# The first group's w_in, fetched and rounded among the first four pieces, with its products from the fourth piece on

## The chip, the cores and the metric

The kernel runs on one core of one Trainium2 chip. The metric is the device time of one execution in microseconds. The kernel before took 1035.81 us, the median of three runs (1035.71 to 1037.92). The profiled execution took 1034.46 us, and its span from the first to the last instruction was 1032.7 us.

## The reference

Two blocks follow each other. The first is a retention layer (attention with a decaying causal mask instead of a softmax), the second a feed-forward layer with the activation h * erf(softplus(h)).

```python
# q, k, v: (8 batches, 8 heads, 576 tokens, 64)
scores = (1 / sqrt(64)) * q @ k.T
Dmat   = where(i >= j, gamma[head] ** (i - j), 0)
x      = (scores * Dmat) @ v                 # -> (4608 tokens, 512)
# w_in: (512, 2048), w_out: (2048, 512)
h   = x @ w_in
sp  = maximum(h, 0) + log1p(exp(-abs(h)))
out = (h * erf(sp)) @ w_out
```

All inputs are random, in float32. The two weights reach the kernel as float64, seen as pairs of 32-bit words, and the kernel rounds them to float32 itself.

## The kernel before

**Attention by pieces.** The 4608 tokens are cut into 36 pieces of 128. A piece goes through three stages: `transposes` (called T below), `scores` (S) and `outputs` (O). Four pieces make a chunk of 512 tokens, which is an input x of the feed-forward layer. There are nine chunks. Pieces 0 to 7 are transposed on TensorE; from piece 8 on VectorE does it (`SQUARES = 8`).

```python
def transposes(i):                       # T(i)
    ...
    for name in "qk":
        pt = ps_at.tile(...)
        for p in range(NP):
            nc.tensor.transpose(pt[:, p, :], ..., ident)
        nc.scalar.copy(out=tT..., in_=pt...)      # qT, kT
    load(i + 2, "q")

def scores(i):                           # S(i)
    ...  # 8 matmuls kT x qT into two PSUM tiles
    for e in range(2):
        tt(sT[:, e], ps[e], mask..., ALU.mult)    # VectorE, "sT"

def outputs(i):                          # O(i)
    ...  # sT x v, and qT x state where a state exists, and k x v for the next state
    scaled(1)                            # VectorE: x <- o
    ...                                  # VectorE: sums; GpSimd: state
    scaled(0)                            # VectorE: x <- o
    load(i + 3, "kv")

stages = [(transposes, 0), (scores, 0)]
for i in range(len(pieces)):
    stages += [(transposes, i + 1), (outputs, i), (scores, i + 1)]
    if i in (PC + 1, 2 * PC - 1):
        stages[-3:-1] = stages[-2], stages[-3]
```

**Weights by parts.** The hidden dimension is cut into four groups. A group has four parts of w_in (tile `wa`) and four of w_out (`wb`), 512 KB each. `load_weights()` asks for the next part; `round_weights(n)` emits the next n steps of the rounding. One part is five steps; after the last part of a tile four more form sums in place.

```python
def load_weights():
    part = next(coming, None)
    if part is not None:
        t = wraw.tile([P, 2 * WP], UINT32, tag="wraw", name="wraw")     # 4 buffers
        for rows, src in part[0]:
            nc.sync.dma_start(out=t[rows]..., in_=src)
        words.append((t, *part[1:]))

def rounding():
        ...
        nc.scalar.activation(a_f, high_f, AF.Abs)                    # step 1, ScalarE
        nc.scalar.mul(out=r_f, in_=low, mul=2.0**-52)
        yield
        nc.vector.tensor_scalar(...)                                 # step 2
        yield
        nc.vector.tensor_scalar(...)                                 # step 3
        yield
        nc.vector.scalar_tensor_tensor(...)                          # step 4
        yield
        nc.vector.tensor_scalar(out=high, ...)                       # step 5
        engine = nc.vector if (name, g) == ("wa", 0) else nc.gpsimd
        engine.tensor_tensor(out=r_f, in0=high_f, in1=r_f, op=ALU.mult)
        engine.tensor_tensor(out=a_f, in0=a_f, in1=r_f, op=ALU.add)
        ...
        yield
        # after a tile's last part: four tt(...) that form the sums
```

So a part of the first group's w_in is two operations on ScalarE and six on VectorE; a part of w_out is two on ScalarE, four on VectorE and two on GpSimd.

**The first chunk's products.** `First.plain()` multiplies the first chunk with the first group's w_in in eight products of four matmuls (128x256 each). The first four need only w_in's first two parts, the last four the other two.

```python
for half, slots in enumerate(((A11, S3), (A12, A22))):
    for n in range(4):
        tok, f = n // 2, n % 2
        ...  # 4 matmuls into acc[n], from wa[slots[f]] and half the chunk's tokens
        if half == 1:
            nc.scalar.copy(out=(self.t2 if tok else self.t1)[:, f], in_=acc[n])
        yield
```

**The opening.** The order of everything up to the end of piece 7's scores is one string: `a` is the next attention stage, `p` one of the eight products (P below), `w` asks for a weight part, a digit is that many steps of rounding, `k` is two matmuls that only keep TensorE busy, `l` loads piece 2's k and v, `c` loads the second half of the constants, `s` stores chunk 0.

```python
load(0)
cst = ...;  nc.sync.dma_start(out=cst[:, :CONST_FIRST], ...)
...
load(1)
...
keep_busy(9)
weigh_values(0)
products = firsts[0].plain()
for what in "alkakakawkakakawaa3awwa2aaa5aawwa5pap5ppwwca4pa5pa5paa5ps1":
    if what == "a":
        attend(done[0] + 1)
    elif what == "p":
        next(products)
    ...
```

**The steady part.** Afterwards first and second products of successive chunks alternate, with attention stages between them as long as there are any. `operands_x` forms the operands of a chunk by four VectorE operations on 128x512.

```python
elif n + 2 < n_s:
    f = firsts[n + 1]
    for step, _ in enumerate(b.middle()):
        attend(min(done[0] + 1, most[0]))
        if step == 0:
            f.erf()
        elif step == 1 and n + 2 >= n_ch:
            operands_x(*order[n + 2])
        ...
    if n + 2 < n_ch:
        attend(after_chunk(n + 2))
        operands_x(*order[n + 2])
```

Of the kernel before, what the change touches and what calls it, by code (L numbers as in the profile page):

```python
# [54 lines left out]
def kernel(  # L55
# [15 lines left out]
    n_ch = n_tok // TCH  # L71
# [26 lines left out]
    def tt(out, in0, in1, op):  # L98
        nc.vector.tensor_tensor(out=out, in0=in0, in1=in1, op=op)  # L99
# [22 lines left out]
    def load_squares(i, name, src):  # L122
        t = raw.tile([P, NP, P * D // SQ], FP32, tag=name + "s", name=f"raw_{name}s", bufs=2)
        for b, s0, n, r0 in pieces[i]:
            m = n // SQ * D
            for part in range(P // SQ):
                e, d0 = part // 2, part % 2 * SQ
                tokens = src[b, e * NP : (e + 1) * NP, s0 : s0 + n, :].rearrange("p (r a) d -> r p (a d)", r=SQ)
                at = r0 // SQ * D
                nc.sync.dma_start(  # L130
                    out=t[part * SQ : (part + 1) * SQ, :, at : at + m - SQ], in_=tokens[:, :, d0 : d0 + m - SQ]
                )
        return t

    def load_rows(i, name, src, bufs):
        if name == "q":
            t = raw.tile([P, NP, P * D // SQ], FP32, tag="qs", name="raw_q", bufs=bufs)
            t = t.rearrange("p a x -> p (a x)")[:, : H * D].rearrange("p (h d) -> p h d", h=H)
        else:
            t = raw.tile([P, H, D], FP32, tag=name, name=f"raw_{name}", bufs=bufs)  # L140
        for b, s0, n, r0 in pieces[i]:
            for e in range(2):
                heads = src[b, e * NP : (e + 1) * NP, s0 : s0 + n, :]
                nc.sync.dma_start(out=t[r0 : r0 + n, e::2, :], in_=heads.rearrange("h p d -> p h d"))  # L144
        return t

    def load(i, names="qkv"):
        if i < len(pieces):
            t = loaded.setdefault(i, {})
            for name in names:  # L150
                src = {"q": q, "k": k, "v": v}[name]
                if name == "q" and i < SQUARES:
                    t["q"] = load_rows(i, "q", q, 2)
                elif name == "q":
                    t["qs"] = load_squares(i, "q", q)
                    t["ks"] = load_squares(i, "k", k)
                elif name == "v" or len(pieces[i]) == 1:
                    t[name] = load_rows(i, name, src, 4)
# [7 lines left out]
    gk, gq, gp, tri, gk2, gq2, tri2 = (cst[:, a:b] for a, b in zip(ends, ends[1:]))  # L166
    gq, gq2 = (g.rearrange("p (a i) -> p a i", a=NP) for g in (gq, gq2))
    gp = gp.unsqueeze(2).to_broadcast([P, NP, D])
    load(1)

# [52 lines left out]
# [3 lines that stand above are left out]
            t = wraw.tile([P, 2 * WP], UINT32, tag="wraw", name="wraw")  # L228
            for rows, src in part[0]:
                nc.sync.dma_start(out=t[rows].rearrange("p (h f) -> p h f", h=2), in_=src)  # L230
            words.append((t, *part[1:]))
# [48 lines left out]
    def round_weights(n=1):  # L280
        for _ in range(n):
            next(round_step, None)

    ident = cpool.tile([P, P], FP32, name="ident")
    make_identity(nc, ident)
    assert S % P == D and 2 * D == P and n_tok == len(pieces) * P and len(pieces) % PC == 0
# [139 lines left out]
    stages = [(transposes, 0), (scores, 0)]  # L426
# [4 lines left out]
    stages = [(of, i) for of, i in stages if i < len(pieces)]  # L431
    done = [0]

    def before_chunk(c):

        return stages.index((outputs, c * PC)) if c < n_ch else len(stages)

    def after_chunk(c):

        return stages.index((outputs, (c + 1) * PC - 1)) + 1  # L440

    def attend(upto):
        while done[0] < min(upto, len(stages)):
            of, i = stages[done[0]]
            of(i)
            done[0] += 1
# [3 lines left out]
    def load_x(g, c):  # L450
        x[g, c] = x_tile()
        nc.sync.dma_start(out=x[g, c][:, :n_dc], in_=xd[c])

    def store_x(c):
        nc.sync.dma_start(out=xd[c], in_=x[0, c][:, :n_dc])

    def operands_x(g, c):
        t = x[g, c]
        b11, b12, b21, b22 = (t[:, 2 * d : 2 * d + 2, h * TH : (h + 1) * TH] for d in range(2) for h in range(2))
        t1, t2, t4 = (t[:, n_dc + j, :].rearrange("p (d i) -> p d i", d=2) for j in range(3))  # L460
        if g == 0 or c == 0:
            tt(t1, b12, b11, ALU.subtract)
            tt(t2, b22, t1, ALU.subtract)
            tt(b12, b22, b12, ALU.subtract)
        else:
            tt(t2, b12, b11, ALU.add)
            tt(t1, b22, t2, ALU.subtract)
        if g == 0:
            store_x(c)
        tt(t4, b21, t2, ALU.subtract)  # L470
        x[g, c] = {A11: b11, A12: b21, S4: b22, A22: t4, S1: t1, S2: t2, S3: b12}
# [211 lines left out]
    order = [(g, c) for g in range(n_g) for c in range(n_ch)]  # L683
# [11 lines left out]
    def keep_busy(n):  # L695
        for _ in range(n):
            nc.tensor.matmul(idle[:, :P], lhsT=ident, rhs=ident, start=True, stop=True)
# [4 lines left out]
    def run(steps, rounds=(), stages=1):  # L702

        for step, _ in enumerate(steps):
            attend(min(done[0] + stages, most[0]))
            round_weights(rounds[step] if step < len(rounds) else 0)
# [4 lines left out]

    for what in "alkakakawkakakawaa3awwa2aaa5aawwa5pap5ppwwca4pa5pa5paa5ps1":
        if what == "a":
            attend(done[0] + 1)
        elif what == "p":
            next(products)
        elif what == "s":
            store_x(0)  # L720
        elif what == "l":
            load(2, "kv")
        elif what == "c":
            nc.sync.dma_start(out=cst[:, CONST_FIRST:], in_=consts[:, CONST_FIRST:])
        elif what == "w":
            load_weights()
        elif what == "k":
            keep_busy(2)
        else:
            round_weights(int(what))  # L730
    firsts[0].softplus()
    most[0] = before_chunk(3)
    attend(after_chunk(1) + 1)
    operands_x(0, 1)
    for step, _ in enumerate(firsts[1].first()):
        attend(done[0] + 1)
# [4 lines left out]
    for b, nxt in zip(blocks[1:], blocks[2:] + [None]):  # L741
        n = order.index((b.g, b.c))
        if isinstance(b, First):
            most_g[0] = order[n - 1][0] + 1
            run(b.middle(), (1, 1) if n != 2 else ())
            firsts[n - 1].sums()
            run(seconds[n - 1].first(), (1, 1) if n > 2 else ())
            run(b.last(), (1,) if 2 < n < n_ch else ())
            if n in (2, 3):
                load_weights()  # L750
            most[0] = before_chunk(n + 3)
# [3 lines that stand above are left out]
                attend(min(done[0] + 1, most[0]))  # L755
                if step == 0:
                    f.erf()
                elif step == 1 and n + 2 >= n_ch:
                    operands_x(*order[n + 2])
                elif step == 2 and n_ch - 4 < n < n_ch:  # L760
                    round_weights()
            if n + 2 < n_ch:
                attend(after_chunk(n + 2))
                operands_x(*order[n + 2])
            run(nxt.first(), (1,) if n > 1 else ())
            f.multiply()
            seconds[n + 1].begin()
            if n_ch <= n + 3 < n_s:
                load_x(*order[n + 3])
            run(b.last(), (0, 1) if n > 1 else ())  # L770
        elif n + 1 < n_s:
            firsts[n + 1].erf()
            seconds[n + 1].begin()
            rest = b.rest()
            for _ in range(3):
                next(rest)
            firsts[n + 1].multiply()
            run(rest)
            firsts[n + 1].sums((0,))
            first = nxt.first()  # L780
            next(first)
            firsts[n + 1].sums((1,))
            run(first)
        else:
            run(b.rest())
# [30 lines left out]
```

## Time and profile before

| What | Value |
|---|---|
| Time, median of three | 1035.81 us |
| Span of the profiled execution | 1032.7 us |
| TensorE busy | 1015.1 us (98%) |
| VectorE busy | 679.1 us (66%) |
| ScalarE busy | 387.8 us (38%) |
| GpSimd busy | 125.4 us (12%) |
| HBM read, written | 119.02 MB, 47.19 MB |

The shares are averages over the whole span. The opening is the first 70 us of it, and there the engines stand otherwise than later, so it has to be read by itself: the span in 40 slices, then the instructions of each engine in order of time. In those lists a row gives start, duration, engine, line, operation and tiles, and in brackets how long the engine was idle before it and what released it. Line 99 is the helper `tt`, so its groups are told apart by their tiles. TensorE is PE, VectorE DVE, ScalarE ACT, GpSimd POOL; SPq is the queue that issues the transfers.

### The profile page before, as it was taken

The numbers are of one execution on the slowest core, as the hardware profiler recorded it, in microseconds if no ns is written. First come the engines' busy times: TensorE is split into PE (matmuls) and PEld (weight loads), VectorE is DVE, ScalarE is ACT, GpSimd is POOL, SyncE is SP. The second block draws the span as 40 slices with busy tenths as digits, with TensorE's granted clock in tenths as the row PEclk, the third lists the DMA queues.
The fourth block names the chain that finished last, engine by engine and source line by source line (L and its number), as shares of the span: only waits on it lengthen the run. The fifth ranks groups of instructions, "written<-read, shape, count | busy, mean of one in ns | idle before, by whom it ended". The sixth has DMA issues, their size and how long they took to land.

```text
span 1032.7 us, 15920 instructions
## 1 busy us (share of the span) xinstructions
PE 1015.1 (98%) x6322; PEld 872.7 (85%) x6322; DVE 679.1 (66%) x1063; ACT 387.8 (38%) x477; POOL 125.4 (12%) x122
## 2 busy tenths in 40 slices
PE   8899999999999999999999999999999999999998
PEld 7777888887888788888888888888888888888887
DVE  3998877877875755666666656666657655555555
ACT  2353134232244444333443344444443333333332
POOL 2161121222211210000001001100100000000000
PEclk9999999999999999999999999999999999999999
DMA  8989979979983544444445344444333334444433
GB/s 192 213 212 228 244 159 241 230 173 247 216 195 131 184 143 143 142 143 165 163 155 169 145 143 143 151 166 153 143 122 122 123 124 131 132 130 133 126 89 116
DMA packets 148778, 167.27 MB, mean 162 GB/s; under 512 B 97632, under 2 KB 123360, under 8 KB 140640
## 3 DMA queue, kind: packets, MB, share of 16 engines
q1 hardware_dynamic: 147696, 165.47, 57.2%
q8 instruction: 50, 0.82, 0.4%
q10 hardware_dynamic: 1008, 0.79, 0.3%
q14 instruction: 24, 0.20, 0.1%
HBM read 119.02 MB, written 47.19 MB: 161 GB/s over the span
## 4 chain that ended last, share of the span: by engine, by line
PE 87%; DVE 4%; SPq 3%; DMA 3%; issue 1%; ACT 1%; POOL 0%; DVEq 0%; ACTq 0%
PE a L591 23%; PE a L483 22%; PE g L483 12%; PE g L591 11%; PE e L591 6%; PE e L483 5%; PE s L339 3%; PE o L357 2%; SPq L144 2%; PE o L380 1%; DMA wraw<-in_moe_w_in_dram 1%; PE o L368 1%; SPq L130 1%; DVE t L99 1%; DMA cst<-in_decays_dram 1%
## 5 line engine op out<-in xcount | busy, mean ns | idle before, releaser
L483 PE MATMUL a<-x,wa 128*128 128x256 f32 x1120 | 266.1, 380 | 0.0
L483 PEld LDWEIGHTS a<-x,wa 128*128 128x128 f32 x1120 | 211.6, 190 | 29.5
L591 PE MATMUL a<-wb,s 128*128 128x256 f32 x864 | 205.7, 381 | 0.0
L591 PEld LDWEIGHTS a<-wb,s 128*128 128x128 f32 x864 | 162.9, 190 | 23.6 <-ACT o L605 0.7
L99 DVE TENSOR_TENSOR t<-g,t 128x512 f32<-128x512 f32 x70 | 48.3, 690 | 150.6 <-ACT t L513 112.9
L483 PE MATMUL g<-x,wa 128*128 128x256 f32 x560 | 133.2, 381 | 2.0 <-DVE o L99 2.0
L483 PEld LDWEIGHTS g<-x,wa 128*128 128x128 f32 x560 | 105.7, 190 | 17.3 <-DVE o L99 2.4
L99 DVE TENSOR_TENSOR o<-a,o 128x512 f32<-128x512 f32 x108 | 74.3, 688 | 50.4 <-PE a L591 50.4
L508 ACT COPY t<-a 128x512 f32<-128x512 f32 x35 | 20.5, 586 | 189.8 <-PE a L483 189.8
L99 DVE TENSOR_TENSOR t<-t,s 128x1024 f32<-128x1024 f32 x72 | 87.8, 1260 | 0.0
L552 ACT ACTIVATE s<-t 128x1024 f32<-128x1024 f32 x72 | 72.1, 1049 | 32.3 <-DVE t L99 32.3
L267 POOL TENSOR_TENSOR wraw<-wraw 128x512 f32<-128x512 f32 x28 | 29.7, 1062 | 434.8 <-DVE wraw L265 182.5
L99 DVE TENSOR_TENSOR x<-x 128x512 f32<-128x512 f32 x116 | 79.7, 720 | 1.2
L519 ACT COPY t<-a 128x512 f32<-128x512 f32 x35 | 20.5, 586 | 151.9 <-PE a L483 151.9
L556 ACT ACTIVATE s<-s 128x1024 f32<-128x1024 f32 x72 | 72.1, 1048 | 0.4
L591 PE MATMUL a<-wb,t 128*128 128x256 f32 x288 | 68.6, 381 | 1.1 <-DVE t L99 1.1
L591 PE MATMUL e<-wb,t 128*128 128x256 f32 x288 | 68.6, 381 | 0.0
L591 PE MATMUL g<-wb,s 128*128 128x256 f32 x288 | 68.6, 381 | 0.0
L591 PE MATMUL g<-wb,t 128*128 128x256 f32 x288 | 68.2, 380 | 0.0
L99 DVE TENSOR_TENSOR o<-g,o 128x512 f32<-128x512 f32 x72 | 49.3, 685 | 28.1 <-ACT o L605 23.3
L483 PE MATMUL e<-x,wa 128*128 128x256 f32 x280 | 66.8, 381 | 0.0
L99 DVE TENSOR_TENSOR sT<-s,cst 128x512 f32<-128x512 f32 x72 | 46.1, 682 | 27.4 <-PE s L339 18.8
(75 smaller groups left out, 1199.9 us busy)
## 6 DMA issues: line engine op xcount, KB each, us to landing
od<-o SPq DMA_DIRECT2D x54, 512.0 KB, 3.6
x<-xd SPq DMA_DIRECT2D x27, 1024.0 KB, 4.8
o<-od SPq DMA_DIRECT2D x27, 1024.0 KB, 5.0
raw_qs<-in_q_dram SPq DMA_DIRECT2D x96, 112.0 KB, 4.7
raw_ks<-in_k_dram SPq DMA_DIRECT2D x96, 112.0 KB, 4.2
xd<-x SPq DMA_DIRECT2D x9, 1024.0 KB, 5.4
raw_k<-in_k_dram SPq DMA_DIRECT2D x64, 128.0 KB, 4.6
raw_v<-in_v_dram SPq DMA_DIRECT2D x64, 128.0 KB, 4.6
```

The lines of the kernel that those rows point to most:

```text
L99: nc.vector.tensor_tensor(out=out, in0=in0, in1=in1, op=op)
L130: nc.sync.dma_start(out=t[part * SQ : (part + 1) * SQ, :, at : at + m - SQ], in_=tokens[:, :, d0 : d0 + m - SQ])
L144: nc.sync.dma_start(out=t[r0 : r0 + n, e::2, :], in_=heads.rearrange("h p d -> p h d"))
L267: engine.tensor_tensor(out=r_f, in0=high_f, in1=r_f, op=ALU.mult)
L339: nc.tensor.matmul(ps[e][:, p, :], lhsT=t["kT"][heads[e], p, :], rhs=t["qT"][heads[e], p, :], start=True, stop=True)
L357: nc.tensor.matmul(o[p % 2][heads[(e + p) % 2], p // 2, :], lhsT=t["v"][:, 2 * p + e, :], rhs=t["sT"][:, e, p, :], start=(p < 2), stop=(no ...
L483: nc.tensor.matmul(acc[:, j * TH : (j + 1) * TH], lhsT=weights["wa", self.g][:, a, d, j * P : (j + 1) * P], rhs=x[self.g, self.c][a][:, d, :],
L508: nc.scalar.copy(out=self.t1[:, 1], in_=self.a)
L519: nc.scalar.copy(out=self.t2[:, 0], in_=self.a)
L552: nc.scalar.activation(self.s[:, j], t, AF.Softplus)
L556: nc.scalar.activation(self.s[:, j], self.s[:, j], AF.Erf)
L591: nc.tensor.matmul(acc[:, tp, :], lhsT=left[:, j * TH + tp * P : j * TH + (tp + 1) * P], rhs=weights["wb", self.g][:, b, j, :], start=(sta ...
```

## The change

The first two parts of w_in are asked for right after the constants, one ahead of piece 1 and one behind it; the other two follow after the first and second outputs. The rounding is spread among the first four pieces. The first chunk's products begin right after the fourth piece's outputs, and then alternate with the stages of pieces 4 to 7, where before they began after the fifth piece's scores and stood partly in a row. The rounding of w_out that stood behind piece 7's scores comes ahead of piece 6's outputs. The aim is to use VectorE while the first pieces are still arriving, and to give TensorE products to do between the stages of attention.

A second edit concerns the steady part: once no stage of attention is left, `operands_x` comes one step earlier, ahead of an addition of the second products. A set records which chunks have been done.

```diff
-    load(1)
 ...
+    load_weights()
+    load(1)
+    load_weights()
     ident = cpool.tile([P, P], FP32, name="ident")
 ...
+    summed = set()
+
     def operands_x(g, c):
+        summed.add((g, c))
 ...
-    for what in "alkakakawkakakawaa3awwa2aaa5aawwa5pap5ppwwca4pa5pa5paa5ps1":
+    for what in "alka1kak4awka1kak4awaa1a4aa1a4pawpawpap4awpa5wpapa5cpa5aa1s":
 ...
-                elif step == 1 and n + 2 >= n_ch:
+                elif step == 1 and (n + 2 >= n_ch or done[0] == len(stages)):
                     operands_x(*order[n + 2])
 ...
-            if n + 2 < n_ch:
+            if order[n + 2] not in summed:
                 attend(after_chunk(n + 2))
                 operands_x(*order[n + 2])
```

Written out with T, S, O and P, r for rounding steps and W for a part asked for, the two strings are:

```
before T0 S0 T1 O0 W S1 T2 O1 W S2 T3 r3 O2 W W S3 r2 T4 O3 S4 r5 T5 O4 W W S5 r5 P O5 P r5 P P
       W W T6 r4 P S6 r5 P T7 r5 P O6 S7 r5 P r1
after  T0 S0 r1 T1 r4 O0 W S1 r1 T2 r4 O1 W S2 T3 r1 O2 r4 S3 T4 r1 O3 r4 P S4 W P T5 W P O4 P r4
       S5 W P O5 r5 W P T6 P S6 r5 P T7 r5 O6 S7 r1
```

Both have the same stages, eight products, 40 rounding steps, matmuls that only keep TensorE busy (not written out here) and the same transfers. Every engine has the same instructions before and after; only their order differs.

## The prediction

> **What bounds the kernel now.** I read the span in 40 slices first, then the busy time of each engine by stretches, then the engines in order of time.
>
> ```profile
> PE   8899999999999999999999999999999999999998
> DVE  3998877877875755666666656666657655555555
> DMA  8989979979983544444445344444333334444433
> ```
>
> From slice 3 on TensorE is the bound. All the change can touch is the first slices, where VectorE goes from 3 tenths to 9 and the DMA engines are full, and single waits later. The stretches of the opening:
>
> ```profile
> core 0: us, PE busy (x) PEld busy (x) DVE busy (x) ACT busy (x) POOL busy (x), PEclk, DMA share, GB/s
> 10.00:24.00 14.00, 13.48 (x200) 11.45 (x198) 5.15 (x11) 4.24 (x8) 3.70 (x4) 1.00 0.95 199
> 24.00:34.00 10.00, 7.59 (x106) 5.87 (x103) 9.69 (x20) 3.40 (x7) 2.27 (x3) 1.00 0.96 176
> 55.00:65.00 10.00, 9.81 (x129) 7.68 (x128) 9.80 (x18) 6.52 (x10) 7.01 (x8) 1.00 0.56 127
> 65.00:80.00 15.00, 12.53 (x116) 9.91 (x115) 14.76 (x20) 5.50 (x7) 8.79 (x7) 1.00 1.02 268
> ```
>
> To 24 us VectorE has two thirds of its time free; from 24 to 80 it has none. This is what the change goes for. But the DMA engines are full in the same first stretch (0.95), so a weight part that comes earlier pushes pieces back. TensorE's rows in order of time:
>
> ```profile
> 9.73 0.63 PE L324 MATMUL pt_q<-ident,raw_q 128*128 128x128 f32 x4 [0.80 <-DMA raw_q<-in_q_dram]
> 10.88 0.63 PE L324 MATMUL pt_k<-ident,raw_k 128*128 128x128 f32 x4 [0.52 <-DMA raw_k<-in_k_dram]
> ...
> 25.16 0.66 PE L324 MATMUL pt_q<-ident,raw_q 128*128 128x128 f32 x4
> ...
> 29.16 1.16 PE L339 MATMUL s<-qT,kT 64*128 64x128 f32 x16
> 32.13 0.63 PE L324 MATMUL pt_q<-ident,raw_q 128*128 128x128 f32 x4 [1.81 <-DMA raw_q<-in_q_dram]
> ...
> 60.48 1.64 PE L357 MATMUL o<-sT,raw_v 128*64 128x128 f32 x16
> ...
> 63.34 1.99 PE L483 MATMUL a<-x,wa 128*128 128x256 f32 x8
> ```
>
> Piece 1 waits for its data at 9.73 and 10.88, T4 is at 25.16, O3 ends at 29.16, O7 runs from 60.48 to 63.34. These are my milestones. (sT is what VectorE makes of S: the two masked tiles that O needs.) VectorE in the late place that the second edit touches, and TensorE's waits there:
>
> ```profile
> 328.35 0.69 DVE L99 TENSOR_TENSOR t<-g,t 128x512 f32<-128x512 f32 x1 [1.07 <-PE g L483]
> 335.37 0.69 DVE L99 TENSOR_TENSOR o<-g,o 128x512 f32<-128x512 f32 x1 [6.33 <-ACT o L605]
> 335.98 0.42 DVE L265 TENSOR_SCALAR wraw<-wb 128x512 uint32<-128x512 uint32 x1
> 336.31 4.44 DVE L99 TENSOR_TENSOR x<-x 128x512 f32<-128x512 f32 x4
> ```
>
> ```profile
> PE g L483 <- DVE o L99: 2.0, 1, 2.0
> PE s L339 <- DVE kT L318: 1.8, 2, 1.3
> ```
>
> VectorE is idle for 6.33 us, and then, behind 4.44 us of operands, holds TensorE up for 2.0 us, once.
>
> **What the Trainium skill says.** "Perfetto Trace Analysis", section "Optimization Strategy", says that a kernel may have regimes with different bounds and may gain by interleaving them; that is the idea here, and the stretches above show the two regimes. The same page, under "Tensor Engine Instruction (MATMUL, LD_WEIGHTS)", says that VectorE, ScalarE and GpSimd work through their instructions strictly in order: a rounding step that has not got its data, or that merely stands ahead, holds all behind it. The trace agrees as far as it goes, each engine's rows run in the program's order. "SBUF — State Buffer", section "SBUF: two separate sides", says that VectorE and GpSimd hold a port pair in turn, for a whole instruction. Here the last operation of a part (line 268) takes 0.69 us alone but 1.45 us at 28.77, where GpSimd weighs values at 28.63. "TensorE: Matmul & The Clock Gate", section "What's actually happening", says that an idle window of about 3.4 us halves the clock; the granted clock is 1.00 in all these stretches, and no run yet shows a drop.
>
> **The change part by part.**
>
> *Arrival.* Before, releases by data give the pace: piece 1's q, k and v at 9.73, 10.88 and 11.95, so about 1.15 us for each 256 KB. The fourth weight part came 2.42 us after the third (ScalarE's first rounding step starts at 37.62 and 40.04, both times released by the transfer), the second 8.12 us after the first with a piece between (23.08, 31.20); I take 2.7 us a part, 1.2 us for q, k or v. From the constants at 8.6 that gives: part 0 at 11.3; piece 1 at 12.5, 13.7, 14.9; part 1 at 17.6; piece 2 at 18.8, 20.0, 21.2; piece 3 at 22.4, 23.6, 24.8; part 2 at 27.5; piece 4 at 28.7, 29.9; part 3 at 33.8; piece 5 at 35.0, 36.2. So T1 comes 2.9 us later than before, T2 and T3 4 to 5 us later. The wait of 1.81 us before T5 goes.
>
> *Rounding among the pieces.* A part takes VectorE 3.6 us (38.76 to 42.35 for the third). Parts 0 and 1 (12.0 to 15.6, and 19.5 to 23.1) fall into time in which TensorE waits for pieces: free, and 7.2 us are gone from the crowded stretch. Part 2 does not: its r4 stands between O2's evictions and S3's masks. With T3 to 25.6, sT2 to 26.1 and O2 to 28.4 (sT's end plus 2.3, as from 26.87 to 29.16 before), its VectorE steps start at 29.2 and take 3.6 plus about 0.5 of port contention; sT3 is through at 34.6 instead of 31.0. TensorE has only T4 (to 30.5) to fill this. O3 ends at about 36.7: 7.5 us later than the 29.16 of before.
>
> *Products between the stages.* From O3's end to O7's start TensorE has eight products of 1.83, four scores of 1.1, three pairs of transposes of 0.9, and O4 (1.65), O5 and O6 (2.25): 14.6 + 4.4 + 2.7 + 6.15 = 27.9 us. Before, this stretch took 60.48 - 29.16 = 31.3 us; so 3.4 us of waits and hidden stalls are to be had, and I give the change most of them: the products stand between S and O and cover the masks. TensorE is at O7 at 36.7 + 27.9 = 64.6. But S6 ends near 58.6 in the same count, sT6 1.3 later at 59.9, and behind it VectorE has two parts of w_out (2.05 us each as from 51.90 to 53.97, more like 2.6 while GpSimd works), O6's evictions (1.0) and sT7 (1.3): 67.4. O7 then ends near 69.5, against 63.34. That is +6.1.
>
> *After the opening.* Before, TensorE loses about 5 us in waits on VectorE between 60 and 85 us (12.53 of 15 busy in one stretch alone). In the new order w_out's third part is through before O7 and GpSimd's share of it too, so the operands at 65.79 (3.92 us, with contention) should take about 3. I count 1.0 back: +5.1.
>
> *The second edit.* The four operations move into the 6.33 us of idle time. Then the additions behind are done when TensorE needs them: -2.0.
>
> *Waits for squares.* At 235 and 275 us S waits 1.3 and 0.5 us for kT, which waits for its transfer. TensorE arriving later may give some of it back: -0.6, a guess.
>
> Sum: +5.1 - 2.0 - 0.6 = +2.5, so 1035.8 + 2.5 = 1038.3. For the chance that I have the arrivals too late I choose 1038.0.
>
> **The rivals.** *VectorE's earlier start pays after all.* If the pieces arrive faster than I count (transfers of weights have larger pieces than those of q, k and v), or sT3 is not held as long, O3 ends at 33 and O7's start is at TensorE's pace, 61 to 62; then VectorE is ahead and up to 5 us of the waits to 85 us vanish. With the second edit that is 1029 to 1031. For it: 7 us of VectorE's work really move to idle time. Against: T4 cannot be before 28.7, when before it was at 25.16, and 27.9 us of products and stages behind it are fixed, so O7 can hardly come earlier than before. *The loss is hidden anyway.* Between 100 and 300 us the transfers are nearly full too; if they set the pace there, neither loss nor gain in the opening reaches the end, and only the 2.0 us remain: 1033.8. Against: TensorE waits for transfers only twice there. *The clock falls.* T1 waits from about 8.9 to 12.5 with nothing between; an idle window could halve the clock for some us: 1040 to 1042.
>
> **Range and chances.** Losses of 3 to 7 us in the opening against 2 of gain put most of the weight between 1036 and 1041; the first rival pulls the lower end down to 1031.5, the clock and a longer VectorE queue the upper one to 1042.5. 2% would be 20.7 us, more than all waits of TensorE in the whole trace (1032.7 - 1015.1 = 17.6), so faster by that much is out, and for slower nothing of the kind is in sight: 0.01, 0.98, 0.01.
>
> **What would show it right or wrong.** T1's q at 12.5 and T4 at 29 or later: arrival right; near 26: wrong. O3's end at 36 to 37, with sT3 right behind part 2's last VectorE step: the held mask is right. O7 ending later than 67: right; at 62 or before, the first rival. No wait of g for an addition near 342: the second edit right. If the opening is as I say and the time is still below 1035, the later waits gave more back than I count, and my last guess is the wrong step.

## The result, and the profile after

The changed kernel took 1041.93 us (median, 1040.58 to 1043.53), beside 1036.38 us for the kernel before in the same comparison: ratio 1.0052, 95% interval [1.0032, 1.0072]. The change makes the kernel slower by about half a per cent. The span of the profiled execution went from 1032.7 to 1040.7 us.

The span in 40 slices, for the rows shown of before, and the granted clock:

```profile
PE   7889999999999999999999999999999999999998
DVE  4669768778778665656666656666666555555555
PEclk9889999999999999999999999999999999999999
DMA  9978979989994444443445444444433333444433
```

VectorE's first three slices went from 3, 9, 9 to 4, 6, 6: some of its work did move into the first, but in the next two it does less than before. TensorE gained nothing by it, its first and third slices fell by a tenth, and the clock, 9 everywhere before, has an 8 in the second and third. The same stretches as before:

```profile
core 0: us, PE busy (x) PEld busy (x) DVE busy (x) ACT busy (x) POOL busy (x), PEclk, DMA share, GB/s
10.00:24.00 14.00, 10.98 (x134) 9.36 (x135) 9.35 (x17) 4.84 (x8) 2.08 (x2) 0.88 1.07 190
24.00:34.00 10.00, 7.09 (x96) 5.30 (x92) 7.71 (x16) 3.58 (x6) 2.27 (x3) 0.95 1.11 199
65.00:80.00 15.00, 11.31 (x125) 8.99 (x124) 10.64 (x20) 6.86 (x9) 7.77 (x8) 0.77 0.95 232
```

From 10 to 24 us VectorE does 9.35 us instead of 5.15, and TensorE 10.98 instead of 13.48, because its pieces are not there yet. From 65 to 80 us neither is full, and the clock is at 0.77. TensorE's rows at the milestones of the prediction:

```profile
12.32 0.96 PE L326 MATMUL pt_q<-ident,raw_q 128*128 128x128 f32 x4 [3.25 <-DMA raw_q<-in_q_dram]
...
30.01 0.66 PE L326 MATMUL pt_q<-ident,raw_q 128*128 128x128 f32 x4
...
34.53 2.37 PE L359 MATMUL o<-sT,raw_v 128*64 128x128 f32 x16 [3.04 <-DVE sT L99]
...
38.95 2.39 PE L542 MATMUL p<-x,wa 128*128 128x256 f32 x8
...
66.20 1.16 PE L341 MATMUL s<-qT,kT 64*128 64x128 f32 x16
71.05 2.52 PE L359 MATMUL o<-sT,raw_v 128*64 128x128 f32 x16 [3.69 <-POOL wraw L266]
```

These are T1, T4, O3, the first product, S7 and O7. Three waits of 3 us and more stand in these rows: T1 for its transfer, O3 for its masks (sT), O7. The last is put down to GpSimd, but what O7 needs is sT, and that comes from VectorE:

```profile
29.45 0.41 DVE L99 TENSOR_TENSOR x<-o,cst 128x256 f32<-128x256 f32 x1
29.78 0.72 DVE L251 TENSOR_SCALAR wa<-wa 128x512 f32<-128x512 f32 x1
...
32.99 0.69 DVE L267 TENSOR_TENSOR wa<-wa,wraw 128x512 f32<-128x512 f32 x1
33.60 1.28 DVE L99 TENSOR_TENSOR sT<-s,cst 128x512 f32<-128x512 f32 x2
...
65.39 0.61 DVE L251 TENSOR_SCALAR wb<-wb 128x512 f32<-128x512 f32 x1 [0.85 <-ACT wb L246]
66.03 1.41 DVE L255 TENSOR_SCALAR wb<-wb 128x512 uint32<-128x512 uint32 x1
67.48 1.41 DVE L259 SCALAR_TENSOR_TENSOR wb<-wraw,wb 128x512 uint32<-128x512 uint32 x1
...
70.27 1.28 DVE L99 TENSOR_TENSOR sT<-s,cst 128x512 f32<-128x512 f32 x2
```

S3 is done at about 30.0 us, and its masks start at 33.60, right behind the third w_in part's last rounding step. At O7 it is the third w_out part. It waits 0.85 us for its first step on ScalarE, and two operations that take 0.43 and 0.69 us elsewhere take 1.41 each, while GpSimd works on the part before and then weighs values:

```profile
65.80 1.36 POOL L267 TENSOR_TENSOR wb<-wb,wraw 128x512 f32<-128x512 f32 x1
67.12 1.22 POOL L307 TENSOR_TENSOR raw_v<-raw_v,cst 128x512 f32<-128x512 f32 x1
```

Last, what the second edit was for. The operands of the last chunk now stand in VectorE's free time:

```profile
338.65 0.69 DVE L99 TENSOR_TENSOR t<-g,t 128x512 f32<-128x512 f32 x1 [1.07 <-PE g L488]
339.26 2.61 DVE L99 TENSOR_TENSOR x<-x 128x512 f32<-128x512 f32 x4
345.68 0.69 DVE L99 TENSOR_TENSOR o<-g,o 128x512 f32<-128x512 f32 x1 [3.80 <-ACT o L610]
```

They take 2.61 us instead of 4.44, and the wait of g for an addition is gone from TensorE's list.

From O7 on TensorE has the same instructions in the same order in both kernels, so the distance between the two can be read at any of them:

| TensorE's instruction | Before, us | After, us | Distance |
|---|---|---|---|
| O7 starts | 60.48 | 71.05 | 10.6 |
| product behind O7 starts | 63.34 | 75.61 | 12.3 |
| first of the second products starts | 79.47 | 90.16 | 10.7 |
| S near 240 us starts | 237.48 | 247.75 | 10.3 |
| g behind the second edit starts | 344.27 | 352.37 | 8.1 |
| span | 1032.7 | 1040.7 | 8.0 |

The loss is made in the first 76 us, and the second edit takes 2 us of it away. The medians differ by less than these two spans (5.6 us): the profiled execution of the kernel before, 1034.46 us, is among its faster ones.

### The profile page after: what moved, and what is told of

Same layout as the page of the kernel before. It is cut to its first block, busy times and chain, and to the rows that moved or that the text cites. A ratio compares the mean times of both kernels' runs of the same rounds, so it can differ in the third digit from the quotient of the medians.

```text
span 1040.7 us, 15926 instructions
## 1 busy us (share of the span) xinstructions
PE 1020.7 (98%) x6322; PEld 877.7 (84%) x6322; DVE 677.4 (65%) x1063; ACT 388.0 (37%) x477; POOL 123.5 (12%) x122
## 4 chain that ended last, share of the span: by engine, by line
PE 90%; DMA 3%; DVE 3%; SPq 2%; issue 1%; ACT 1%; POOL 0%; DVEq 0%
PE a L596 23%; PE a L488 22%; PE g L596 12%; PE g L488 11%; PE e L596 6%; PE e L488 6%; PE s L341 3%; PE o L359 3%; PE o L382 1%; PE o L370 1%; DMA raw_v<-in_v_dram 1%; SPq L130 1%; PE p L542 1%; DMA raw_ks<-in_k_dram 1%; SPq L144 1%
## 5 line engine op out<-in xcount | busy, mean ns | idle before, releaser
L513 ACT COPY t<-a 128x512 f32<-128x512 f32 x35 | 20.5, 586 | 189.2 <-PE a L488 189.2
L99 DVE TENSOR_TENSOR x<-x 128x512 f32<-128x512 f32 x116 | 76.5, 692 | 1.2
L524 ACT COPY t<-a 128x512 f32<-128x512 f32 x35 | 20.5, 586 | 151.9 <-PE a L488 151.9
```

Source lines behind the costliest of these rows:

```text
L513: nc.scalar.copy(out=self.t1[:, 1], in_=self.a)
L524: nc.scalar.copy(out=self.t2[:, 0], in_=self.a)
```

## The experiments

My theory after the trace: three kinds of cost in the opening. The transfers of early parts hold the pieces back; the third w_in part's rounding ahead of S3's masks, and the third w_out part's ahead of O6's evictions and S7's masks, each hold TensorE up for over 3 us; and behind each long wait the clock is at half for some us. The rivals: that only the arrival costs, that the total of VectorE's work is what binds and the order does not matter, or that the clock is only a sign. All ratios are to the kernel before. The changed kernel's own, 1.0052, comes from four executions and is known to 2 thousandths, so a gain against it is clear of noise only from about 2.3 thousandths on.

**The second edit alone**, on the kernel before.

```diff
-elif step == 1 and n + 2 >= n_ch:
+elif step == 1 and (n + 2 >= n_ch or done[0] == len(stages)):
```

> The kernel before with only the second edit (the operands of the last chunk one step earlier). My theory: the 2.0 us wait of a first product for an addition near 342 us vanishes and nothing takes its place, so 2.0 us under the kernel before (ratio 0.998). The rival, that a wait taken away so early in a stretch bound by TensorE comes back as another wait, gives 1.000.

Measured: 0.9976 [0.9966, 0.9985], 1034.24 us beside 1036.85. So 2.5 us less, with the interval from 1.6 to 3.5; the wait is gone and nothing replaced it.

**Masks ahead of the third w_in part**, on the changed kernel.

```diff
-T3 r1 O2 r4 S3 T4 r1 O3 r4
+T3 r1 O2 S3 r4 T4 r1 O3 r4
```

> The changed kernel with the masks of S3 ahead of the third w_in part's four rounding steps, nothing else. My theory: O3 no longer waits 3.0 us behind rounding; it starts near 31.5 instead of 34.5 us and, without the idle time ahead of it, at full clock, so it ends near 34 instead of 39.0; at the start of O7 4 to 5 us remain of that, at the end 3.5 to 5 us against the changed kernel (ratio to before about 1.001). The rival, that the total of VectorE's work sets when O7 can start and the wait there only grows, gives under 1.5 us of gain.

Measured: 1.0024 [1.0013, 1.0035]. That is 2.8 thousandths, 2.9 us, under the changed kernel. TensorE's rows of O3, O4 and O7:

```profile
32.02 1.09 PE L359 MATMUL o<-sT,raw_v 128*64 128x128 f32 x16
...
43.23 1.53 PE L359 MATMUL o<-sT,raw_v 128*64 128x128 f32 x15 [1.36 <-issue]
...
67.93 2.52 PE L359 MATMUL o<-sT,raw_v 128*64 128x128 f32 x16 [3.68 <-POOL wraw L266]
```

O3 starts 2.5 us earlier and takes no stretch of half clock. O7 is 3.1 us earlier, where I had expected 4 to 5, and the gain at the end is under the 3.5 us that I had named: O4 now waits 1.36 us, for its masks stand behind the fourth part's rounding. O7's own wait has not grown (3.68 beside 3.69), so VectorE's total is not what sets it.

**The third w_out part behind S7**, on the changed kernel.

```diff
-T7 r5 O6 S7 r1
+T7 O6 S7 r5 r1
```

> The changed kernel with the third w_out part's rounding behind piece 7's scores, where it was before the change, instead of ahead of piece 6's outputs. My theory: O7's wait of 3.7 us falls under 1 us and O7 runs at full clock, so it ends near 71 instead of 75.6 us; VectorE then has the part's 2 to 4 us still to do, so 1.5 to 3 us of gain at the end against the changed kernel (ratio to before about 1.003). The rival, that the place does not matter because VectorE's queue is the bound from there to 95 us, gives no gain.

Measured: 1.0025 [1.0015, 1.0034], 2.7 thousandths under the changed kernel. O7 and the product behind it:

```profile
67.06 1.64 PE L359 MATMUL o<-sT,raw_v 128*64 128x128 f32 x16 [0.82 <-POOL raw_v L307]
69.84 1.99 PE L488 MATMUL a<-x,wa 128*128 128x256 f32 x8
```

The wait went from 3.69 to 0.82 us, and the next product starts 5.8 us earlier (69.84 beside 75.61); 1.1 us of this stood already at S7 (65.07 beside 66.20), before the edit can act. In this profile the distance is still there at the end (spans of 1034.7 and 1040.7 us). But it is the fastest of the 22 executions (1036.49 us, median 1039.32); the medians leave about half.

**Both reorderings.**

> Both reorderings together. If the two waits are separate costs, the gains add: about 6 us against the changed kernel, the level of the kernel before (ratio 0.999 to 1.001). If one wait hides behind the other, it is no better than the better of the two alone. If the late arrival of the pieces is what costs, and the waits only show it, the ratio stays over 1.003.

Measured: 0.9987 [0.9979, 0.9995]. From 1.0052 that is 6.5 thousandths; the two alone sum to 5.5, which agrees within the uncertainty. More closely, without the 1.0052: where one of the two is done, the other still brings 3.7 or 3.8 thousandths (1.0024 and 1.0025 to 0.9987, each to about 1.4). They are separate costs. What is left over the second edit alone is 0.9987 - 0.9976 = 1.1 thousandths, about 1.1 us, with an uncertainty of 1.2.

**The waits filled**, on the changed kernel: matmuls into a spare tile while TensorE waits. The work that counts is in the same order.

```diff
-alka1kak4awka1kak4awaa1a4aa1a4p...1s
+alka1kkkkkkkkak4awka1kak4awaa1a4aa1kkkkkka4p...1sf
+elif what == "f":
+    fill = ps_a.tile([P, W], FP32, tag="a", name="fill")
+    for _ in range(16):
+        nc.tensor.matmul(fill[:, :P], lhsT=ident, rhs=ident, start=True, stop=True)
```

> The changed kernel with matmuls that only keep TensorE busy put into its three longest waits (14 ahead of T1, 12 ahead of O3, 16 ahead of O7); the order of all other work is unchanged. If the half clock that stands in the profile around 33 to 39 and 70 to 77 us is a cost of its own, it goes: O3, the first product, O7 and the product after it run at full speed, O7 ends about 4 us earlier, and 2 to 4 us of that are left at the end against the changed kernel (ratio to before 1.002 to 1.0035). If the clock is only a sign and VectorE's queue sets the pace, the time stays within 1 us of the changed kernel (ratio about 1.005).

Measured: 1.0034 [1.0024, 1.0044], 1.8 thousandths under the changed kernel, just under the 2 us of my theory's lower end. The granted clock (PEclk) in the changed kernel:

```profile
33.00:39.00 6.00, 4.47 (x49) 3.58 (x49) 2.30 (x4) 1.21 (x2) 1.04 (x1) 0.50 1.03 173
70.00:77.00 7.00, 5.95 (x51) 4.70 (x52) 3.17 (x9) 0.38 (x1) 3.08 (x5) 0.54 1.09 279
```

and with the waits filled:

```profile
20.50:23.70 3.20, 2.90 (x18) 2.71 (x20) 1.61 (x3) 0.59 (x1) 1.30 (x1) 0.56 0.95 210
33.00:39.00 6.00, 5.82 (x77) 5.30 (x78) 3.78 (x8) 1.83 (x3) 1.19 (x1) 1.00 0.93 148
70.00:77.00 7.00, 6.46 (x78) 5.02 (x77) 4.92 (x12) 1.78 (x2) 3.43 (x4) 1.00 1.13 273
```

The two stretches are at full clock, O7 and the product behind it start at 70.40 and 73.17 us instead of 71.05 and 75.61. From O7's start to the product behind it there are 2.77 us instead of 4.56, so the half clock costs time of its own. The 1.8 thousandths, 1.9 us, are not clear of noise by themselves, but the executions of this kernel point the same way: the five with a mean clock of 1.000 average 1037.7 us, the nine with 0.998 1040.9 us. How large the whole cost is stays open, for a wait for piece 2 that I had not filled took the half clock instead, at 20.5 to 23.7 us, and O1 began in it.

**Early parts alone**, on the kernel before.

```diff
-    load(1)
 ...
+    load_weights()
+    load(1)
+    load_weights()
-alkakakawkakakawaa3a...
+alkakakakakakaaa3a...
```

> The kernel before with only the first two w_in parts asked for as early as in the changed kernel (around piece 1); rounding, products and the second edit as before. My theory: T1 starts near 12.3 instead of 9.7 us and T4 near 30 instead of 25.2, the wait before T5 goes, so 2 to 4 us are lost by O4, of which VectorE, full anyway until 85 us, takes part: 1 to 3 us over the kernel before (ratio 1.001 to 1.003). The rival, that the pieces' arrival is hidden behind VectorE, gives 1.000; a third, that the arrival is most of the loss, gives over 1.004.

Measured: 1.0020 [1.0011, 1.0029], 2.1 us. T1, T4 and T5:

```profile
11.74 0.63 PE L326 MATMUL pt_q<-ident,raw_q 128*128 128x128 f32 x4 [2.36 <-DMA raw_q<-in_q_dram]
...
28.96 0.66 PE L326 MATMUL pt_q<-ident,raw_q 128*128 128x128 f32 x4
...
34.18 0.66 PE L326 MATMUL pt_q<-ident,raw_q 128*128 128x128 f32 x4 [0.38 <-DVE x L99]
```

T4 is at 28.96 instead of 25.16 us and T5 at 34.18 instead of 32.13. The arrival costs about 2 us and is neither hidden nor the most of it. The clock has a share in this too: behind T1's wait it is at half (0.51 here), while O0 runs.

```profile
13.00:16.40 3.40, 3.40 (x24) 3.17 (x26) 0.00 (x0) 0.59 (x1) 1.04 (x1) 0.51 1.07 179
```

**Parts behind the pieces**: the kernel before with the second edit and an opening that keeps the two ideas of the change, early rounding and spread products, but asks for the parts behind pieces 2, 3, 4 and 5 and rounds each w_in part behind a piece's masks, up to the third.

```
T0 W S0 T1 O0 W S1 T2 r1 O1 W S2 r4 T3 r1 O2 W S3 r4 T4 r1 O3 S4 P r4 T5 r1 W P O4 r4 P W S5 P r4 P
O5 W r5 P T6 W P S6 r5 P T7 O6 S7 r5 r1
```

> The kernel before with the second edit and another opening: w_in's first part is asked for behind piece 2, the second behind piece 3, the third and fourth behind pieces 4 and 5; each is rounded behind a piece's masks, not ahead of them; the products start after piece 4's scores and alternate with the stages, and the third w_out part is rounded behind piece 7's scores. If pieces first and masks first are what matters, and the early rounding and the spread products are sound ideas, T1 to T3 start as before, O7 starts at 58 to 60 us instead of 60.5 and the waits to 85 us shrink: 3 to 5 us under the kernel before (ratio 0.995 to 0.997), less than the second edit alone takes. If the opening is bound by VectorE's total, it is as fast as the second edit alone (0.9976).

Measured: 0.9964 [0.9952, 0.9976] in five executions. But the profile did not say where it came from: O7 started at 61.3 us, no earlier than before. So I ran it again beside the second edit alone on one chip.

> The kernel before with the second edit alone, again, beside the three below on one chip. Ratio 0.997 to 0.9985 as before.

Measured: 0.9972 [0.9962, 0.9982], 1032.73 us beside 1035.49.

> The opening with the parts behind the pieces, again. Its first profile had O7 at 61.3 us, no earlier than the 60.5 of the kernel before, and the position at 80 us was the same within 0.3 us; by that it should be no faster than the second edit alone (within 0.1% of it). If its first ratio of 0.9964 was the opening's doing, it is 1 to 2 us faster than the second edit alone again.

Measured: 0.9976 [0.9967, 0.9985] in 22 executions. So the first ratio does not hold as a gain of this opening: it is as fast as the second edit alone. In both profiles TensorE waits at T4 (2.43 us in the first, 1.54 and 1.75 us in the second), where it did not wait before, and O3 behind it runs at half clock. So a cost of arrival is still in it, and whether the early rounding and the spread products would bring something without that is not shown.

**w_out one place up.** Each w_out part is rounded one place further up, the first two directly behind each other ahead of S6. The fourth part, so far finished after the opening, now falls into it as well.

```diff
-P O5 W r5 P T6 W P S6 r5 P T7 O6 S7 r5 r1
+r1 P O5 W W r4 r1 P r4 T6 P S6 r1 r4 P T7 O6 S7 r1 r4
```

> As the opening with the parts behind the pieces, with each w_out part's rounding one place further up, in VectorE's free time before S6 and O6. If the waits from 65 to 83 us come from VectorE's queue, they shrink by about the 2 us of one part: 1 to 2 us under the run without it. If they come from the order inside that stretch, nothing changes.

Measured: 0.9996 [0.9984, 1.0007], 2 thousandths worse than without it. GpSimd's rows ahead of O6, and O6:

```profile
56.20 1.04 POOL L267 TENSOR_TENSOR wraw<-wraw 128x512 f32<-128x512 f32 x1 [1.15 <-DMA raw_qs<-in_q_dram]
57.31 1.42 POOL L268 TENSOR_TENSOR wb<-wb,wraw 128x512 f32<-128x512 f32 x1
58.70 1.22 POOL L305 TENSOR_TENSOR raw_v<-raw_v,cst 128x512 f32<-128x512 f32 x1
```

```profile
59.97 2.04 PE L357 MATMUL o<-sT,raw_v 128*64 128x128 f32 x16 [2.34 <-POOL raw_v L305]
```

GpSimd weighs piece 6's values behind two rounding operations of 2.5 us, and O6 waits 2.34 us for them. It is the same fault as in the change, on another engine. It is not alone: with the fourth part done early, its four sums now stand ahead of a piece's transposes on VectorE, and TensorE waits 1.89 us for kT. How the 2 thousandths divide is not shown.

```profile
76.46 3.33 DVE L99 TENSOR_TENSOR wb<-wb 128x512 f32<-128x512 f32 x4
82.12 1.16 PE L339 MATMUL s<-qT,kT 64*128 64x128 f32 x16 [1.89 <-DVE kT L318]
```

**Second w_in part behind piece 4.** The second part is asked for behind piece 4, the third and fourth behind piece 5, and the products come from S5 on. The rounding of w_out is not that of the last run: as in the opening with the parts behind the pieces, the third part stands behind S7 and the fourth only begins there. So that opening (0.9976) is the one to compare with.

```
T0 W S0 T1 O0 S1 T2 r1 O1 W S2 r4 T3 O2 W W S3 T4 r1 O3 S4 r4 T5 r1 O4 S5 r4 P r1 P W O5 r4 W P P r4 r1
W W T6 P S6 r4 r1 P T7 r4 P O6 S7 r1 r4 r1 P
```

> As the last, with w_in's second part behind piece 4 and the third and fourth behind piece 5, so that no piece waits for a part that is not needed yet; the products start after S5. If the arrival of pieces 4 and 5 is the rest of the loss in the opening, O7 starts at 58 to 59.5 us and the time is 1 to 2 us under that of the last. If the products' later start leaves new waits, it is no faster.

Measured: 0.9983 [0.9974, 0.9992]. TensorE's longest waits in the trace have no transfer of pieces 4 or 5 among them any more, but:

```profile
PE p L540 <- DVE wa L268: 1.8, 2, 1.0
PE pt_q L324 <- DVE x L99: 1.2, 1, 1.2
```

Products wait for their own rounding, and O7 is at 60.66 us, about where it was before (60.48). It is 1.3 thousandths under the last run, but no better than the second edit alone.

No opening is faster, clear of noise, than the kernel before with the second edit and its own opening: 0.9976 and 0.9972 in two comparisons.

## Why the prediction was right, and where it was short

The range (1031.5 to 1042.5) held the result and the direction was right, by the mechanism it named. The middle, 1038.0, was 3.9 us too low: the change was put at about 2 us and measured at 5.6. The result lies 0.6 us inside the upper end, which had been set for the clock and a longer VectorE queue, and both of these came.

- **Arrival: right.** T1's q at 12.32 for 12.5, T4 at 30.01 for 29 or later. The parts came at 11.27, 18.22, 28.72 and 36.93 for 11.3, 17.6, 27.5 and 33.8; only the fourth was 3 us late.
- **The mask held behind the third part: right.** sT3 is through at 34.88 for 34.6 (in the kernel before at 26.87). O3's end was predicted at 36.7 and was 38.95. The term that was short is O3 itself: it took 4.42 us, where O2 had 2.78 (26.14 to 28.92), because it ran at half clock.
- **Products between the stages: right in size.** 27.9 us from O3's end to S7's end were counted; the trace has 38.95 to 67.3, which is 28.4. I gave the change "most of" 3.4 us of stalls; the wait at O7, which the prediction had too, took them back. (In the kernel before the first product stands behind S5, the scores of the sixth piece, at 36.34 us.)
- **O7: right in kind, short in size.** Predicted to end at 69.5 (+6.1), it ended at 75.6 (+12.3). Of the 6.1 us missing, half clock makes 1.6 in O3, 0.5 in the first product (2.31 from start to start, 1.83 in full speed), and 1.7 in O7 (4.56 beside 2.86): 3.8. Of the other 2.3, 1.6 lie in the two w_out parts: I had counted 5.2 us for both, 1.1 of it for contention with GpSimd, and they took 6.8 (62.47 to 69.27). 0.85 of the 1.6 is the wait for ScalarE, which I had not counted; about 0.8 is VectorE being slower still beside GpSimd, two operations at 1.41 us where they have 0.43 and 0.69. The last 0.7 is spread over sT3, O3 and O7.
- **Given back after the opening: too low.** 1.0 predicted; 1.6 by the first second product, and 0.4 more by the waits at 240 us, where 0.6 had been the guess. TensorE's idle time between 60 and 85 us in the kernel before is under 4 us, not about 5.
- **The second edit: right.** 2.0 predicted, 2.2 in the trace, 1.6 to 3.5 by the run of it alone.

So the largest missing term, 3.8 of 6.1 us, is one that I had put among the rivals and not into the sum. "The clock falls" named 1040 to 1042 us and only T1's wait; the result was 1041.93, and the waits that I had predicted myself at O3 and O7 are long enough for the same thing. The rival that VectorE's earlier start pays fell for this change, and the later openings, without the two reorderings, show no gain from it either. That the loss is hidden by transfers until 300 us fell too: 10.3 of 10.7 us were still there near 247 us.

What the runs leave open: how the 1.1 thousandths between the doubly reordered kernel and the second edit alone divide. Early arrival alone costs 2.0, so the spread products and the early rounding may bring 0.9 back, but the intervals (about one thousandth each) do not tell this from nothing. Why no opening has O7 before about 60.5 us in its profile was not taken apart.

## What to carry to other kernels

An engine that works in order takes its work in the order of emission, so free time on it is only worth something ahead of what the bound engine waits for: work that can wait belongs behind the masks, not ahead of them, and the same fault cost about 2.9 us in one place and 2.8 us in another, each uncertain by over 2 us, and on GpSimd a wait of 2.3 us. Where transfers are full, asking earlier for one thing delays another; ask who needs what first. When a prediction contains a wait of 2 us or more on TensorE, count the clock behind it as well, or fill the wait.

## What the runs showed of the hardware

The Trainium skill, "TensorE: Matmul & The Clock Gate", section "What's actually happening", puts the idle window that halves the clock at about 3.4 us. Here shorter waits had half clock behind them as well. In the thirteen profiles each of the 14 waits of TensorE from 2.05 to 3.69 us was followed by it within 4 us. Of twelve waits from 1.45 to 2.04 us, seven were and five were not. The wait of g for an addition, which the second edit removes, shows both. In the kernel before it is 2.04 us long and the clock stays at 1.00 (PEclk is the third number from the end):

```profile
344.27 1.99 PE L483 MATMUL g<-x,wa 128*128 128x256 f32 x8 [2.04 <-DVE o L99]
345.20:348.70 3.50, 3.50 (x18) 3.06 (x18) 0.59 (x2) 0.58 (x1) 0.00 (x0) 1.00 0.98 324
```

With the early parts alone it is 2.03 us long, the clock falls to half, and the product behind it takes 3.19 us instead of 1.89:

```profile
346.17 2.42 PE L485 MATMUL g<-x,wa 128*128 128x256 f32 x8 [2.03 <-DVE o L99]
348.39 3.19 PE L485 MATMUL a<-x,wa 128*128 128x256 f32 x8
347.50:351.00 3.50, 3.50 (x11) 2.77 (x10) 0.14 (x1) 0.00 (x0) 0.00 (x0) 0.51 0.96 329
```

So below some 2 us the length of a wait does not decide it alone; what else does is not shown. The clock also goes with the spread between executions of one kernel: the four of the changed kernel have mean clocks from 0.991 to 0.998, and of 61 executions of the kernel before in one comparison the 17 with a mean clock of 1.000 average 1034.3 us, the four with 0.995 1037.3 us.
